# Loads in the order of use, and another share-out of the LayerNorm statistics, at the start of a fused attention and MLP kernel

## Chip, cores, metric

One core of one Trainium2 chip. The metric is device time in microseconds (us). A profiled span is about 1.7 us shorter than the device time of the same execution. All runs named here are single-core runs that were recorded as fast. The experiments ran in three sets of rounds, each set on another chip, always with the kernel before in the same rounds; a comparison across sets is weaker than one within a set.

## The reference, cut to what matters

```python
x  = A_x                                   # 2048 tokens x 1024 channels
xn = layernorm(x)
out = x + attention(xn, wq, wk, wv, wo, beta) + mlp(xn, w1, b1, w2, b2)

def mlp(xn, w1, b1, w2, b2):               # mixes tokens, not channels
    h = layernorm(xn)                      # the second layernorm
    u = gelu(h.T @ w1 + b1)                # 2048 -> 3584
    return (u @ w2 + b2).T
```

Only the start matters here: x is read in 16 chunks of 128 tokens; each chunk needs its mean and variance, a reciprocal square root and a scaling before PE (TensorE) can multiply it by w1. The MLP's contraction runs over tokens, so each chunk of h is one step of a sum that eight PSUM banks hold.

## The kernel before

The first four blocks of 128 hidden units are computed while x is still coming in: for each chunk c, eight matmuls (four w1 blocks, two halves of h) accumulate into the eight banks, 128 "early matmuls" in all. The other 24 blocks follow without a break.

```python
for q in range(4):                                  # loads, all issued by SP
    for c0, n in (((0, 1), (1, 1), (2, 2)) if q == 0 else ((4 * q, 4),)):
        self.load_x(c0, n)                          # 2 KB rows
        if c0 != 2:
            self.load_w1_rows(c0 if q == 0 else 0, q)   # 4 chunks, 256 columns: 512-byte rows
    if q:
        self.load_w1_rows(1, q)
# [...] beta, b1 and b2 are loaded by ACT's queue before that; beta is 64 bytes, sent to all 128 partitions

NORM_ORDER = ("D0 A1 S0 h0 A1' D2 S1 B1 g1 S2 h2 D3 A4 A4' S3 h3 D5 S4,5 D6 B4,5 g4 g5 A7 A7' D8 S6,7 B6,7 g6 g7 "
              "D9 A10 A10' S8,9 D11 B8,9 g8 g9 S10,11 D12 B10,11 g10 g11 A13 A13' D14 S12,13 D15 B12,13 g12 g13 "
              "S14,15 B14,15 g14 g15")
# Dc   statistics of chunk c on DVE: bn_stats, bn_stats, bn_aggr
# Ac   sum on ACT and two small scalings;  Ac'  sum of squares on ACT
# Sc   two small DVE steps, then the square root on ACT
# hc   h of chunk c on DVE;  Bc gc  a bias on DVE, then h on POOL
# [...] the bias columns b1c, b2c are transposed by PE and copied by ACT after S0

for c in range(N_TCH - 2):
    self.early_hidden(c, c + 1, range(8))           # eight matmuls on chunk c
for b in range(8):
    self.early_hidden(N_TCH - 2, N_TCH, (b,))       # chunks 14 and 15, bank by bank
```

Every engine works through its own instructions in this order. A word that stands early in the string can therefore hold up everything behind it on its engine.

The softmax here doesn't subtract the row's maximum and nothing guards it: scores larger than these inputs give would overflow.

## Time and profile before

| | before |
|---|---|
| device time, median | 721.3 us, 3 runs, before the prediction; 721.57 us (720.23 to 722.08, 4 runs: the same three and one more) in the comparison |
| profiled span | 720.2 us |
| first early matmul starts | 10.79 us |
| early matmuls end | 45.48 us |
| x of chunk 1 / of chunks 2 and 3 has landed | 8.22 / 11.16 us |

128 matmuls of 0.216 us are 27.6 us of work, so about 18 of the first 45.5 us are start-up, waiting and slow clock.

The page's head, kernel before: span, then busy time of each engine with its share and its number of instructions. PE is the engine that is always busy.

```profile
span 720.2 us, 11218 instructions
PE 701.0 (97%) x4818; PEld 324.6 (45%) x4818; DVE 263.1 (37%) x577; ACT 276.7 (38%) x314; POOL 111.1 (15%) x151
```

The timeline of PE, kernel before: start, length, engine, line, operation, output<-input, count; in brackets the idle time before and what ended it.

```profile
10.79 1.86 PE L192 MATMUL ps_all<-h,w1s_78 128*128 128x512 bf16 x4 [3.53 <-DVE h L647]
...
23.08 1.02 PE L192 MATMUL ps_all<-h,w1s_78 128*128 128x512 bf16 x4 [2.74 <-POOL h L651]
23.94 1.75 PE L192 MATMUL ps_all<-h,w1s_79 128*128 128x512 bf16 x4
25.48 1.91 PE L192 MATMUL ps_all<-h,w1s_78 128*128 128x512 bf16 x4
...
45.48 13.98 PE L192 MATMUL ps_all<-h,w1s_80 128*128 128x512 bf16 x64
```

Four matmuls take 1.02 us at full clock (the line at 23.08) and 1.7 to 1.9 us at the slow clock that follows the two long waits; it can set in a little later, as here at 23.94. The line at 45.48 is the first of the steady stage (the third w1 tile), so its start is the end of the early matmuls.

The timeline of ACT and DVE, kernel before, three lines:

```profile
8.24 1.06 ACT L615 ACTIVATE junk<-xin 128x1024 bf16<-128x1024 bf16 x1 [5.94 <-DMA xin<-in_A_x_dram]
...
9.98 0.55 DVE L647 TENSOR_SCALAR h<-xin,ln_mv,ln_rs 128x1024 bf16<-128x1024 bf16 x1 [4.25 <-ACT ln_rs L635]
...
32.38 1.01 DVE L633 TENSOR_SCALAR ln_rs<-ln_mv 128x2 f32<-128x2 f32 x1
```

ACT waits for x of chunk 1 until 8.24. The square root of chunk 0 stands behind that in ACT's order, so h of chunk 0 starts at 9.98. The last line is a step on two numbers per partition that takes 0.17 us elsewhere; here it takes 1.01, until the POOL h that was running ends.

The stretches view, kernel before: the stretch and its length, busy time of PE, PEld, DVE, ACT and POOL, granted PE clock, DMA share, GB/s.

```profile
5.00:10.00 5.00, 1.87 (x6) 0.49 (x4) 0.65 (x5) 1.70 (x8) 0.00 (x0) 1.00 0.88 266
...
25.00:30.00 5.00, 5.00 (x19) 2.04 (x18) 4.75 (x12) 2.76 (x7) 3.09 (x4) 0.75 0.21 53
```

From 5 to 10 us every compute engine idles most of the time. From 25 to 30 us PE is always busy, at 0.75 of its clock on average, and DVE is nearly as busy (4.75 of 5 us).

The chain of waits, kernel before (start, length, what):

```profile
2.74 8.42 DMA xin<-in_A_x_dram
...
21.73 1.21 POOL h L651
22.94 0.14 issue
23.08 24.94 PE ps_all L192 x107
```

It goes from the landing of x of chunks 2 and 3 over DVE and ACT to POOL's h of chunk 4, and from 23.08 us on over PE alone.

### The profile page before, as it was taken

Reading aid. Unit: us, or ns where it says so; the run is one execution under the profiler, and the core shown is the slowest. Engines: PE = TensorE matmul, PEld = TensorE weight load, DVE = VectorE, ACT = ScalarE, POOL = GpSimd, SP = SyncE. Lnnn points to the kernel's source line nnn. Section 1 sums busy time; section 2 is a strip of 40 time slices with the busy share of each in tenths; the row PEclk is TensorE's granted clock in tenths of the full one; section 3 lists DMA queues with packets and bytes.
Section 4 is the critical chain, followed back from the end, with each engine's and each line's share of the span. In section 5 each row is a group of like instructions: output and inputs, shape, how many; then the busy total and the mean of one; then the engine's idle time right before and its main releaser. Section 6 shows DMA issues by size and latency. Waiting matters only on the chain.

```text
span 720.2 us, 11218 instructions
## 1 busy us (share of the span) xinstructions
PE 701.0 (97%) x4818; PEld 324.6 (45%) x4818; DVE 263.1 (37%) x577; ACT 276.7 (38%) x314; POOL 111.1 (15%) x151
## 2 busy tenths in 40 slices
PE   6899999999999999999999999999999999999996
PEld 2344444444444444444444444444444444444442
DVE  4970000000002343344444545544555544344452
ACT  4551122111225445445444444443444444434420
POOL 1540000000001112211221111222111122111220
PEclk9999999999999999999999999999999999999999
DMA  9549677246016373872654625355352635527103
GB/s 269 142 115 177 144 190 192 64 112 124 12 60 163 66 125 87 127 118 63 123 117 87 126 44 126 75 109 120 79 125 45 126 86 97 111 53 117 30 27 114
DMA packets 211515, 77.17 MB, mean 107 GB/s; under 512 B 172554, under 2 KB 203274, under 8 KB 211466
## 3 DMA queue, kind: packets, MB, share of 16 engines
q1 hardware_dynamic: 211248, 76.43, 48.9%
q8 instruction: 38, 0.62, 0.4%
q14 instruction: 11, 0.09, 0.0%
q10 hardware_dynamic: 218, 0.02, 0.0%
HBM read 59.79 MB, written 5.24 MB: 90 GB/s over the span
## 4 chain that ended last, share of the span: by engine, by line
PE 93%; DVE 3%; ACT 2%; DMA 1%; issue 1%; SPq 0%; POOL 0%; DVEq 0%; ACTq 0%
PE ps_all L192 93%; DMA xin<-in_A_x_dram 1%; ACT etmp_1584 L749 1%; DVE kT_1570 L746 0%; DVE ln_st L606 0%; DVE kT_1572 L746 0%; DVE kT_1571 L746 0%; DVE ln_st L605 0%; ACT pT L786 0%; SPq L214 0%; DVE h L647 0%; ACT L749 0%; POOL h L651 0%; DVE fin_7771 L1016 0%; DVE fin_7770 L1016 0%
## 5 line engine op out<-in xcount | busy, mean ns | idle before, releaser
L786 ACT ACTIVATE pT<-ps_all 128x1536 bf16<-128x1536 f32 (+1 forms) x96 | 153.0, 1593 | 96.8 <-PE ps_all L192 96.8
L792 POOL TENSOR_SCALAR_AFFINE_SELECT pT<-pT 128x512 bf16<-128x512 bf16 x128 | 90.9, 723 | 561.5 <-ACT pT L786 561.5
L708 ACT ACTIVATE gT<-ps_all,b1c 128x512 bf16<-128x512 f32 x56 | 37.7, 689 | 134.5 <-PE ps_all L192 134.5
L192 PE MATMUL ps_all<-h,w1s_78 128*128 128x512 bf16 x320 | 73.9, 385 | 7.1 <-POOL h L651 3.5
L192 PE MATMUL ps_all<-h,w1s_79 128*128 128x512 bf16 x320 | 73.8, 385 | 0.0
L746 DVE CAST kT_1570<-ps_all 128x512 bf16<-128x512 f32 x11 | 7.6, 690 | 178.9 <-PE ps_all L192 178.9
L192 PE MATMUL ps_all<-gT,w2h_912 128*128 128x512 bf16 x224 | 56.3, 380 | 0.0
L192 PE MATMUL ps_all<-gT,w2h_914 128*128 128x512 bf16 x224 | 56.3, 380 | 0.0
L192 PE MATMUL ps_all<-h,w1s_80 128*128 128x512 bf16 x256 | 55.9, 379 | 0.0
L192 PE MATMUL ps_all<-gT,w2h_913 128*128 128x512 bf16 x224 | 53.9, 381 | 0.0
L192 PE MATMUL ps_all<-gT,w2h_911 128*128 128x512 bf16 x224 | 53.9, 381 | 0.0
L192 PEld LDWEIGHTS ps_all<-h,w1s_78 128*128 128x128 bf16 x320 | 31.4, 99 | 46.3 <-issue 8.5
L192 PEld LDWEIGHTS ps_all<-h,w1s_79 128*128 128x128 bf16 x320 | 31.7, 99 | 39.0 <-issue 2.3
L826 DVE CAST ost_1579<-ps_all 128x264 bf16<-128x264 f32 (+1 forms) x64 | 23.8, 394 | 69.2 <-PE ps_all L192 69.0
L826 DVE CAST ost_1580<-ps_all 128x264 bf16<-128x264 f32 (+1 forms) x64 | 23.8, 394 | 69.0 <-PE ps_all L192 68.9
L192 PEld LDWEIGHTS ps_all<-h,w1s_80 128*128 128x128 bf16 x256 | 25.0, 98 | 30.2
L749 ACT ACTIVATE etmp_1584<-ps_all 128x512 bf16<-128x512 f32 x24 | 14.3, 597 | 58.1 <-DVE kT_1572 L746 20.7
L192 PEld LDWEIGHTS ps_all<-gT,w2h_912 128*128 128x128 bf16 x224 | 20.6, 98 | 25.2 <-issue 2.5
L192 PEld LDWEIGHTS ps_all<-gT,w2h_914 128*128 128x128 bf16 x224 | 20.5, 98 | 24.7 <-issue 2.5
L192 PEld LDWEIGHTS ps_all<-gT,w2h_911 128*128 128x128 bf16 x224 | 19.3, 98 | 25.3 <-issue 6.4
L192 PEld LDWEIGHTS ps_all<-gT,w2h_913 128*128 128x128 bf16 x224 | 19.3, 98 | 25.3 <-issue 6.4
L192 PE MATMUL ps_all<-wo_sb,oT_1587 128*128 128x512 bf16 x128 | 30.2, 379 | 0.0
(154 smaller groups left out, 815.3 us busy)
## 6 DMA issues: line engine op xcount, KB each, us to landing
w1s_80<-in_B_w_dram SPq DMA_DIRECT2D x4, 1024.0 KB, 5.9
w1s_78<-in_B_w_dram SPq DMA_DIRECT2D x4, 1024.0 KB, 5.6
w1s_79<-in_B_w_dram SPq DMA_DIRECT2D x4, 1024.0 KB, 5.7
wq_907<-in_A_wq_dram SPq DMA_DIRECT2D x16, 256.0 KB, 3.5
wq_908<-in_A_wq_dram SPq DMA_DIRECT2D x16, 256.0 KB, 3.6
wk_909<-in_A_wk_dram SPq DMA_DIRECT2D x16, 256.0 KB, 3.8
wk_910<-in_A_wk_dram SPq DMA_DIRECT2D x16, 256.0 KB, 4.0
w2h_911<-in_B_w_dram SPq DMA_DIRECT2D x8, 448.0 KB, 4.8
```

What stands on the lines that cost most here:

```text
L192: ins = self.nc.tensor.matmul(*args, **kwargs)
L708: fw.op("act", lambda e: e.activation(self.gT[:, fc, half * 512:(half + 1) * 512], self.bank(b), ACT.Gelu_apprx_tanh, bias=self.b1c[:, fc: ...
L746: fw.op("dve", lambda e: e.tensor_copy(self.kT[k][:], self.bank(b)), reads=[self.R_bank[b]], writes=[self.R_kT[k]])
L749: fw.op("act", lambda e: e.activation(self.etmp[1][:], self.bank(b), ACT.Exp), reads=[self.R_bank[b]], writes=[self.R_etmp[1]])
L786: fw.op("act", lambda e: e.activation(self.pT[:, :, off:off + total], self.ps[:, 0:4, 0:total], ACT.Exp, scale=SCALE), reads=self.R_bank[0:4],
L792: fw.op("pool", lambda e: e.affine_select(d, d, pattern=[[0, 4], [1, P]], compare_op=ALU.is_ge, fill=0.0, base=0, channel_multiplier=-1), ...
L826: fw.op("dve", lambda e: e.tensor_copy(dst, self.ps[:, b, 0:n * VW]), reads=[self.R_bank[b]], writes=[self.R_ost[o][qb]])
```

## The change

The intent: PE should get its first h earlier, the w1 columns should come with longer rows and in the order in which they are used, and no engine should hold up the chain. Chunks 1, 3, 5, 8, 11 and 14 get their statistics from ACT (before: 1, 4, 7, 10, 13). The first five h and the last one are DVE's, ten h are POOL's (before: 13), and the bias copies move to DVE.

```diff
+        self.w1early = nc.alloc_sbuf_tensor_at("w1early", [P, N_TCH, 512], BF16, offset=w1_at)
@@ loads
-        for q in range(4):
-            for c0, n in (((0, 1), (1, 1), (2, 2)) if q == 0 else ((4 * q, 4),)):
-                self.load_x(c0, n)
-                ...
+        for kind, c0, n in (("x", 0, 1), ("x", 1, 1), ("w", 0, 2), ("x", 2, 2), ("w", 2, 2), ("x", 4, 2), ("x", 6, 2),
+                            ("w", 4, 4), ("x", 8, 4), ("w", 8, 4), ("x", 12, 4), ("w", 12, 4)):
+            if kind == "x":
                 self.load_x(c0, n)
+            else:
+                self.fw.dma(self.w1early[:, c0:c0 + n, :], self.B_w1[c0 * P:(c0 + n) * P, 0:512]...)
@@ bias columns
-            fw.op("act", lambda e: e.activation(col[:], self.bank_bf(b)[:, 0:n], ACT.Copy),
+            fw.op("dve", lambda e: e.tensor_copy(col[:], self.bank_bf(b)[:, 0:n]),
@@ order of work (C: the bias columns)
-    NORM_ORDER = ("D0 A1 S0 h0 A1' D2 S1 B1 g1 S2 h2 D3 A4 A4' S3 h3 D5 S4,5 D6 B4,5 g4 g5 ... g14 g15")
+    NORM_ORDER = ("D0 A1 S0 h0 C A1' S1 h1 A3 D2 S2 h2 A3' D4 S3 h3 A5 S4 h4 A5' D6 S5 B5 g5 S6 D7 B6 g6 A8 A8' S7 D9 "
+                  "B7 g7 S8,9 D10 B8,9 g8 g9 A11 A11' D12 S10,11 D13 B10,11 g10 g11 S12,13 A14 A14' D15 B12,13 g12 g13 "
+                  "S14,15 B14,15 g14 h15")
@@ early matmuls: wait for the w1 rows of the chunk alone, read w1early
```

More of the change, by code (lines that the diff above doesn't have):

```diff
@@ L421, in alloc @@
         self.h = e.take("h", [P, N_TCH, D_MODEL], BF16)
+        w1_at = (e.at + 31) // 32 * 32
         self.w1ring = [e.take(f"w1s{i}", [P, N_TCH, 256], BF16) for i in range(3)]
+        self.w1early = nc.alloc_sbuf_tensor_at("w1early", [P, N_TCH, 512], BF16, offset=w1_at)
         self.late_end = e.at
@@ L516, in consts @@
             self.w1_ring.srcs.append(self.B_w1[:, fp * 256:(fp + 1) * 256].rearrange("(c p) f -> p c f", p=P))
-        self.R_w1q = [[Res(f"w1q{i}_{q}") for q in range(4)] for i in range(2)]
-        for q in range(4):
-            for c0, n in (((0, 1), (1, 1), (2, 2)) if q == 0 else ((4 * q, 4),)):
+        self.R_w1e = [Res(f"w1e{c}") for c in range(N_TCH)]
+        for kind, c0, n in (("x", 0, 1), ("x", 1, 1), ("w", 0, 2), ("x", 2, 2), ("w", 2, 2), ("x", 4, 2), ("x", 6, 2),
+                            ("w", 4, 4), ("x", 8, 4), ("w", 8, 4), ("x", 12, 4), ("w", 12, 4)):
+            if kind == "x":
                 self.load_x(c0, n)
-                if c0 != 2:
-                    i = c0 if q == 0 else 0
-                    self.load_w1_rows(i, q)
-            if q:
-                self.load_w1_rows(1, q)
+            else:
+                self.fw.dma(self.w1early[:, c0:c0 + n, :],
+                            self.B_w1[c0 * P:(c0 + n) * P, 0:512].rearrange("(c p) f -> p c f", p=P),
+                            writes=self.R_w1e[c0:c0 + n])
         self.w1_ring.issued = 2
@@ L548, in load_x @@
                     writes=[self.R_xin[c] for c in range(c0, c0 + n)])
-    def load_w1_rows(self, i, q):
-        rows = self.B_w1[4 * q * P:4 * (q + 1) * P, i * 256:(i + 1) * 256]
-        self.fw.dma(self.w1ring[i][:, 4 * q:4 * q + 4, :], rows.rearrange("(c p) f -> p c f", p=P),
-                    writes=[self.R_w1q[i][q]])
     def late_consts(self):
@@ L571, in late_consts @@
               reads=[self.R_gcol, self.R_gate], writes=[self.R_gate])
-    NORM_ORDER = ("D0 A1 S0 h0 A1' D2 S1 B1 g1 S2 h2 D3 A4 A4' S3 h3 D5 S4,5 D6 B4,5 g4 g5 A7 A7' D8 S6,7 B6,7 g6 g7 "
-                  "D9 A10 A10' S8,9 D11 B8,9 g8 g9 S10,11 D12 B10,11 g10 g11 A13 A13' D14 S12,13 D15 B12,13 g12 g13 "
-                  "S14,15 B14,15 g14 g15")
+    NORM_ORDER = ("D0 A1 S0 h0 C A1' S1 h1 A3 D2 S2 h2 A3' D4 S3 h3 A5 S4 h4 A5' D6 S5 B5 g5 S6 D7 B6 g6 A8 A8' S7 D9 "
+                  "B7 g7 S8,9 D10 B8,9 g8 g9 A11 A11' D12 S10,11 D13 B10,11 g10 g11 S12,13 A14 A14' D15 B12,13 g12 g13 "
+                  "S14,15 B14,15 g14 h15")
     def norm_and_first_hidden(self):
         for word in self.NORM_ORDER.split():
+            if word == "C":
+                self.bias_columns()
+                continue
             kind, cs = word[0], [int(v) for v in word[1:].rstrip("'").split(",")]
@@ L592, in norm_and_first_hidden @@
                 self.scale_h(c, kind == "h")
-            if word == "S0":
-                self.bias_columns()
         self.rstd(0, N_TCH, 0)
@@ L656, in early_hidden @@
         fw = self.fw
-        q = c0 // 4
-        reads = [self.R_w1q[i][q] for i in range(2)] + self.R_w1s[0:2] + self.R_h[c0:c1]
+        reads = self.R_w1e[c0:c1] + self.R_w1s[0:2] + self.R_h[c0:c1]
         with fw.group(reads=reads, writes=[self.R_bank[b] for b in banks]):
@@ L661, in early_hidden @@
                 fc, half = b // 2, b % 2
-                w = self.w1ring[fc // 2]
                 for c in range(c0, c1):
-                    fw.mm(self.bank(b), w[:, c, (fc % 2) * P:(fc % 2 + 1) * P],
+                    fw.mm(self.bank(b), self.w1early[:, c, fc * P:(fc + 1) * P],
                           self.h[:, c, half * 512:(half + 1) * 512], start=(c == 0), stop=(c == N_TCH - 1))
```

## The prediction

> **What bounds the kernel now.** The page gives PE 97% busy of a 720.2 us span, and the chain that ended last is 93% PE. The change touches only the first 45 us; what this stage wins or loses should be shifted into the end time one for one. The timeline of PE: the first matmul on h starts at 10.79 us, chunk 1 follows at 14.98, chunks 2 and 3 end at 20.3, then PE waits 2.74 us for h of chunk 4 (released by POOL) and runs from 23.08 us until the 128 early matmuls end at 45.48. 128 matmuls at 0.216 us are 27.6 us; the other 18 us are start-up, idle or slow clock, the most there is to win.
>
> **Where these go.**
> 1. x of chunk 1 lands at 8.2 us (ACT starts on it at 8.24), amid 512-byte w1 rows; from 4 to 7 us the DMA moves 130 to 145 GB/s, later 310 to 400. ACT is in order, so chunk 0's square root waits behind chunk 1's sums, and h0 starts at 9.98 though its statistics were done at 5.4.
> 2. Later DVE bounds: 4.5 to 4.8 us busy of each 5 between 15 and 35 us. A chunk's statistics cost DVE 1.66 us, a rstd step 0.4, h 0.55; on ACT statistics cost 2.9; POOL's h costs 1.20.
> 3. Small DVE steps (rstd, bias) wait until a running POOL h ends: 0.46, 0.89, 0.62, 1.01 us instead of 0.11 to 0.17. The Trainium skill, page "SBUF — State Buffer" (SBUF: two separate sides), calls the ports that DVE and GpSimd share an exclusive lock for the whole instruction; the trace agrees.
> 4. After idles of 3.5 and 2.7 us matmuls took 0.43 us for about 3.3 us: 1.7 us lost after 23 us. The skill's page "TensorE: Matmul & The Clock Gate" (Part 1) re-throttles after an idle window of about 3.4 us; here 2.74 sufficed.
>
> **What the change does.** x0 and x1 go first, then w1 in 1 KB rows in order of use. A 512-byte packet takes 27 ns, a 2 KB one 84; I estimate 45 for 1 KB, so the early 6 MB get only about 1 us shorter; order matters more. I expect x1 by 5 us, h0 by 7, the first early matmul at 7 to 8.5, chunk 2 at 12 to 13.5. Statistics on ACT rise from 5 to 6 chunks (1.7 us off DVE); five h go to DVE early in place of three (1.1 us on), plus the last one beside POOL's h14, saving about 1 us at the end; POOL's fall from 13 to 10. The bias copies leave ACT.
>
> Placing these durations in the new order by hand, I get h14/h15 at about 35.5 to 37.5 us (before 40.0) and the early matmuls ending at 41 to 43 us instead of 45.48, with short PE gaps (0.4 to 1.9 us), so probably no slow clock. The gain is 2.5 to 5 us, all of it on the critical path.
>
> **Predicted time:** 717.4 us, range 714.0 to 720.2. Chances: faster by over 2% 0.01, within 2% 0.98, slower 0.01.
>
> **Right if:** matmuls on the third w1 tile start near 42 us; the first early matmul before 9; PE's gaps shrink; after that only a shift.
>
> **Wrong if:** x1 or the first w1 rows still land at 8 us or later (h0 stays near 10.5, gain near zero); the one-chunk steps for chunks 5 to 7 make DVE and POOL alternate; many short gaps keep the clock low; or DMA and clock go free and the gain reaches 7 us.

## The result, and the profile after

The changed kernel takes 717.69 us in the median (717.58 to 717.85, 4 runs), against 721.57 us for the kernel before. The ratio is 0.9949, 95% interval 0.9932 to 0.9967. A ratio is the mean time of one kernel's fast runs over that of the other's in the same rounds, so it is not quite the ratio of the medians. The profiled span fell from 720.2 to 716.0 us.

The page's head, changed kernel:

```profile
span 716.0 us, 11137 instructions
PE 693.5 (97%) x4728; PEld 323.9 (45%) x4818; DVE 259.8 (36%) x583; ACT 279.3 (39%) x320; POOL 107.8 (15%) x148
```

Some matmul records are missing in this trace (4728 of 4818), so PE's busy sum is not compared; starts and ends are.

The timeline of PE, changed kernel:

```profile
6.95 3.61 PE L192 MATMUL ps_all<-h,w1early 128*128 128x512 bf16 x16 [0.48 <-DVE b2c L545]
13.15 6.83 PE L192 MATMUL ps_all<-h,w1early 128*128 128x512 bf16 x23 [2.59 <-DVE h L646]
20.92 5.58 PE L192 MATMUL ps_all<-h,w1early 128*128 128x512 bf16 x24 [0.94 <-POOL h L650]
26.65 3.61 PE L192 MATMUL ps_all<-h,w1early 128*128 128x512 bf16 x16 [0.15 <-POOL h L650]
30.85 10.53 PE L192 MATMUL ps_all<-h,w1early 128*128 128x512 bf16 x47 [0.58 <-POOL h L650]
41.22 13.98 PE L192 MATMUL ps_all<-h,w1s_80 128*128 128x512 bf16 x62
```

The early matmuls start at 6.95 instead of 10.79 and end at 41.22 instead of 45.48. That is 4.26 us, and the spans differ by 4.2: what this stage won was handed on whole. Both figures are of one pair of executions; the timed runs of the comparison give 3.7 us (from the ratio). A wait of 2.59 us and a slow clock are still there (the line at 13.15: 24 matmuls, of which 23 have records, take 6.8 us instead of 5.2).

The timeline of ACT and DVE, changed kernel (its line numbers are one lower than before in this part):

```profile
4.33 1.06 ACT L614 ACTIVATE junk<-xin 128x1024 bf16<-128x1024 bf16 x1 [2.03 <-DMA xin<-in_A_x_dram]
...
6.08 0.55 DVE L646 TENSOR_SCALAR h<-xin,ln_mv,ln_rs 128x1024 bf16<-128x1024 bf16 x1 [0.38 <-ACT ln_rs L634]
...
26.70 1.00 DVE L632 TENSOR_SCALAR ln_rs<-ln_mv 128x2 f32<-128x2 f32 x1
```

The stretches view, changed kernel:

```profile
5.00:10.00 5.00, 4.52 (x21) 1.84 (x20) 2.18 (x10) 2.36 (x8) 0.00 (x0) 1.00 0.80 264
```

Between 5 and 10 us the DMA still moves 264 GB/s, as before (266); from 10 to 15 us it moves 380.

The chain of waits, changed kernel:

```profile
2.19 7.93 DMA xin<-in_A_x_dram
...
29.26 0.21 DVE ln_mv L606
29.47 0.04 DVE ln_nb L638
29.50 0.09 issue
29.59 1.21 POOL h L650
30.80 0.05 issue
30.85 1.25 PE ps_all L192 x5
```

This is the finding of the comparison. Before, PE bounded the stage from 23.08 us on. After, the chain stays on DVE (with short visits to ACT) until 29.5 us, and PE bounds only the last 10 us. The chain still begins with x of chunks 2 and 3, which lands at 10.12 us: 7.93 us after its issue, though x0 and x1, with half the bytes each, took 2.8 and 3.1.

The trace of single DMA packets (one record for each piece of a row that is moved) says where that time is. Ten 2 KB packets that start between 4.2 and 4.7 us, when x0 and x1 are in and x of chunks 2 and 3 is on its way, take 1.8 to 2.6 us each; a usual one takes 0.084. The same holds before: in the first 8 us, 20 packets longer than 0.7 us, 24.4 us in sum over 16 DMA engines, and 14 with 25.8 us after. The ACT queue's load of beta, 128 packets of 64 bytes, runs in the same stretch: its packets start between 5.0 and 9.3 us, and the ten long ones end between 6.1 and 7.3. The long ones thus begin up to 0.8 us before beta's first packet; they only end while beta's packets run.

### The profile page after: what moved, and what is told of

The parts are those of the page before. It is cut to its first block, busy times and chain, and to the rows that moved or that the text cites. A ratio compares the mean times of both kernels' runs of the same rounds, so it can differ in the third digit from the quotient of the medians.

```text
span 716.0 us, 11137 instructions
## 1 busy us (share of the span) xinstructions
PE 693.5 (97%) x4728; PEld 323.9 (45%) x4818; DVE 259.8 (36%) x583; ACT 279.3 (39%) x320; POOL 107.8 (15%) x148
## 4 chain that ended last, share of the span: by engine, by line
PE 91%; DVE 4%; ACT 2%; issue 1%; DMA 1%; SPq 0%; POOL 0%; DVEq 0%; ACTq 0%
PE ps_all L192 91%; DMA xin<-in_A_x_dram 1%; ACT etmp_1595 L746 1%; DVE ln_st L605 1%; DVE ln_st L604 1%; DVE kT_1581 L743 0%; DVE kT_1583 L743 0%; DVE kT_1582 L743 0%; ACT pT L783 0%; DVE ln_mv L606 0%; DVE ln_rs L632 0%; ACT L746 0%; SPq L214 0%; POOL h L650 0%; DVE fin_7782 L1013 0%
## 5 line engine op out<-in xcount | busy, mean ns | idle before, releaser
L192 PE MATMUL ps_all<-gT,w2h_925 128*128 128x512 bf16 x211 | 55.0, 380 | 1.0 <-issue 0.5
L192 PE MATMUL ps_all<-h,w1s_80 128*128 128x512 bf16 x251 | 55.6, 379 | 0.3
L192 PE MATMUL ps_all<-h,w1s_79 128*128 128x512 bf16 x251 | 55.6, 379 | 0.3
L192 PE MATMUL ps_all<-h,w1s_78 128*128 128x512 bf16 x250 | 55.6, 379 | 0.3
L192 PE MATMUL ps_all<-gT,w2h_923 128*128 128x512 bf16 x211 | 54.4, 379 | 1.4 <-issue 1.1
L192 PE MATMUL ps_all<-gT,w2h_924 128*128 128x512 bf16 x220 | 53.7, 381 | 0.2
L192 PE MATMUL ps_all<-gT,w2h_922 128*128 128x512 bf16 x221 | 53.6, 380 | 0.3 <-issue 0.2
L192 PEld LDWEIGHTS ps_all<-h,w1s_80 128*128 128x128 bf16 x256 | 25.0, 98 | 30.2
L192 PEld LDWEIGHTS ps_all<-h,w1s_78 128*128 128x128 bf16 x256 | 25.0, 98 | 30.2
L192 PEld LDWEIGHTS ps_all<-h,w1s_79 128*128 128x128 bf16 x256 | 25.0, 98 | 30.2
L192 PE MATMUL ps_all<-h,w1early 128*128 128x512 bf16 x126 | 30.0, 393 | 4.9 <-DVE h L646 2.6
```

The costliest lines, as they stand in the source:

```text
L192: ins = self.nc.tensor.matmul(*args, **kwargs)
```

## The experiments

My theory A: the gain has two parts, earlier landing and a better order of work; after the change DVE is the bound until 31 us, so the clock and the row length are off the critical path. Its rivals are named in each text. Later theory F was added: beta's tiny packets hold up the large ones. Twelve kernels ran. The diffs below are shortened. Where a time in us follows from a ratio, it is (1 - ratio) times the mean of the kernel before in the same rounds.

### Loads alone

The changed kernel with the old order of work:

```diff
-    NORM_ORDER = (new)      bias copies on DVE at C
+    NORM_ORDER = (old)      bias copies on ACT after S0
```

> Only the loads are new; the order of statistics and h is the old one, bias copies on ACT. Theory A (two parts that add up: the earlier landing of x starts the DVE chain about 1 us earlier, the new order of work gives the rest): x1 lands by 4.5 us, first early matmul near 7 to 8 us, chunk 2 and 3 of x near 10.1 us, h of chunk 4 about 1 us earlier than before's 22.9, early matmuls end at 44 to 44.8 us, span about 719.3. Rival B (the loads are the whole gain): end of the early matmuls near 41.2 us, span 716.

Measured: 719.68 us median (718.87 to 721.84), ratio 0.9994 (0.9976 to 1.0013), so 0.4 us. In the profile x1 lands at 4.16 and the first early matmul starts at 8.18, but then PE waits. The timeline of PE, loads alone:

```profile
8.18 1.90 PE L192 MATMUL ps_all<-h,w1early 128*128 128x512 bf16 x8 [1.03 <-DMA w1early<-in_B_w_dram]
14.35 7.87 PE L192 MATMUL ps_all<-h,w1early 128*128 128x512 bf16 x24 [4.27 <-POOL h L650]
```

In the old order the small steps of chunk 1 (S1) stand behind D2 on DVE, so h of chunk 1 waits for x of chunk 2, though x1 was there six us before. This profiled span was 717.9, lower than expected, but other runs of this kernel had spans up to 720.1. The timed gain is under 1 us, as theory A had it. Rival B, that the loads are the whole gain, is out.

### Order of work alone

The kernel before with the new string and the bias copies on DVE; loads as before.

```diff
-    NORM_ORDER = (old)      bias copies on ACT after S0
+    NORM_ORDER = (new)      bias copies on DVE at C
```

> Only the order of statistics and h is new, with the bias copies on DVE; the loads are the old ones. Theory A: h0 stays near 10 us, x2,3 land at 11.2, so the same DVE chain as after the change runs about 1.1 us later: early matmuls end at 42 to 43 us, span about 717.2. Rival B (loads are the whole gain): end near 45.5, span 720.

Measured: 719.22 us median (718.67 to 721.04), ratio 0.9984 (0.9969 to 0.9999), so 1.2 us; profiled span 717.9. x1 lands at 8.01, the first early matmul starts at 10.65. Theory A is right in kind and too high in size: I had expected about 3 us. Which part of the new order counts was not separated, but for the last h (below). Loads and order together look worth more than their sum (0.4 + 1.2): in the same rounds the changed kernel with the filler of the next experiment, which is as fast as the changed kernel, gained 2.8. This surplus of 1.2 us is not shown by the times, since each of the three figures is uncertain by 1.0 to 1.3 us. The trace of the loads alone gives the reason to expect it: the new order can use an early x1, the old one can't.

### Zeros in PE's wait, after the change

```diff
+        k = {2: 11}.get(c0, 0)                      # ahead of chunk 2
+        with fw.group(reads=[self.R_warm], writes=[self.R_bank[0]]):
+            for _ in range(k):                      # adds zero to bank 0
+                fw.mm(self.bank(0), self.warm[:, 0:P], self.warm[:], start=(c0 == 0), stop=(c0 == 0))
```

> The changed kernel with 11 matmuls on zeros put into PE's 2.6 us wait for chunk 2, so that the clock stays fast. Theory A (after the change the chain in this stage runs over DVE until 30.8 us and the slow clock at 13 to 17 us is off it): slow matmuls vanish, the early matmuls still end within 0.3 us of 41.2, span 716 +- 0.4. Rival C (slow clock is still paid): span falls by 1.5 to 1.9 us.

Measured: 717.65 us median (716.92 to 719.04), ratio 0.9961; the median is that of the changed kernel. No slow matmul is left after the first 6 us. The profiled span is 715.2, 0.8 below the changed kernel's and so 0.4 outside what I had allowed: x of chunks 2 and 3 landed at 9.31 in this execution instead of 10.12, and the chain moved by as much. The slow clock after the change costs nothing; rival C is out.

### Zeros in PE's waits, before the change

The same in the kernel before:

```diff
+        k = {0: 15, 1: 10, 4: 11}.get(c0, 0)        # ahead of chunks 0, 1 and 4
```

> The kernel before with matmuls on zeros put into PE's waits for chunks 0, 1 and 4 (15, 10, 11), so that the clock stays fast. Theory A (PE is the bound from 23.08 us on, and the slow clock after the wait is paid): early matmuls end 1.4 to 1.8 us earlier, near 43.9, span about 718.6. Rival D (DVE bounds before as well, down to the last h at 40.0): gain under 0.5 us.

Measured: 720.68 us median (719.63 to 721.25), ratio 0.9999 (0.9985 to 1.0012): no gain. The profiled span was 717.9, which alone would have looked like a success. The timeline of PE of this kernel:

```profile
19.52 2.54 PE L192 MATMUL ps_all<-warm 128*128 128x512 bf16 x11
22.42 25.84 PE L192 MATMUL ps_all<-h,w1s 128*128 128x512 bf16 x116 [0.37 <-POOL h L651]
```

The slow matmuls are gone, and chunk 4 came 0.66 us earlier because x of chunks 2 and 3 had landed 0.64 us earlier in this execution. Six timed runs do not bear out the expected 1.4 to 1.8 us, although the slow clock was gone in all of them: their mean granted clock is 0.997 to 0.998, that of the kernel before in the same rounds 0.990 to 0.995. The number is the one that rival D had forecast, but its reason is not seen: in the profiled execution PE runs without a wait from 22.42 us on. So my reading that the slow clock costs the kernel before 1.7 us holds for the one profiled execution at most. What it costs in a typical run, and how far the filler itself delays PE when h comes early, stays open.

### 512-byte rows in the new order

```diff
-                self.fw.dma(self.w1early[:, c0:c0 + n, :], self.B_w1[rows, 0:512]...)
+                for i in range(2):
+                    self.fw.dma(self.w1half[i][:, c0:c0 + n, :], self.B_w1[rows, i * 256:(i + 1) * 256]...)
```

> The changed kernel with its new order of loads, but each w1 load split into two of 512-byte rows. Theory A (order counts, row length does not, since from 10 us on DVE bounds and not the DMA): span within 0.5 us of the changed kernel's 716.0. Rival E (1 KB rows count): x of the later chunks lands 1 us or more later and the span is 1 us or more longer.

Measured: 716.99 us median (716.59 to 718.21), ratio 0.9948: no slower than the changed kernel. The profiled span of 715.2 is 0.3 below the band, with x of chunks 2 and 3 at 9.40. The 1 KB rows contribute nothing to the gain that these runs can show; what the new loads give comes from their order.

### The last h back on POOL

```diff
-                  "S14,15 B14,15 g14 h15")
+                  "S14,15 B14,15 g14 g15")
```

> The changed kernel with only the last h back on POOL. The prediction had counted about 1 us for it. Theory A (by then PE is behind: the last h on DVE is ready at 35.0 us, POOL's h14 at 36.1, PE wants both near 37.8): span within 0.3 us of the changed kernel. Rival: 0.5 to 1 us longer.

Measured: 717.89 us median (717.48 to 718.54), ratio 0.9959; profiled span 716.2. The same as the changed kernel within the scatter. The 1 us that I had counted for this piece is not there.

This run shows something about the clock as well. The timeline of PE, last h on POOL:

```profile
13.35 1.89 PE L192 MATMUL ps_all<-h,w1early 128*128 128x512 bf16 x8 [2.86 <-DVE h L646]
```

After 2.86 us of idling the clock is full (8 matmuls in 1.89 us). In the changed kernel 2.59 us sufficed to slow it. The clock records of the 14 kept traces say what differs. In each of them the clock changes only on a grid of 3.41 us. On this grid, PE was busy for 5 to 38% of each of the 11 windows at full clock that were followed by half clock, and for 44% or more of every window that was not (2,886 windows at full clock, busy by the matmul records). The 2.59 us fall mostly into one window, which was 35% busy; the 2.86 us are split over two, 66 and 50% busy.

### Beta late

```diff
-        fw.dma(self.beta_sb[:], self.A_beta.partition_broadcast(P), writes=[self.R_beta], issuer="act")
@@ after the last of the early loads, on SP
+        fw.dma(self.beta_sb[:], self.A_beta.partition_broadcast(P), writes=[self.R_beta])
```

> The changed kernel with the load of beta (128 packets of 64 bytes) issued after all big early loads. In the changed kernel x2,3 lands at 10.1 us, though 11 packets of it that start at 4.2 to 4.7 us take about 2 us each. Theory F (beta's tiny packets hold up the 16 engines): those long packets vanish, x2,3 lands at 7.5 to 8.5 us, the DVE chain starts about 2 us earlier, the span falls by 1.5 to 2.5 us. Rival G (the stall is not caused by the tiny packets): x2,3 still near 10 us, span unchanged within 0.4.

Measured: 715.85 us median, five runs from 715.74 to 715.89, ratio 0.9929 (0.9912 to 0.9946). x of chunks 2 and 3 lands at 7.32 us (expected: 7.5 to 8.5). Two packets longer than 0.7 us are left in the first 8 us, 1.8 us in sum instead of 25.8. The stretches view, beta late:

```profile
5.00:10.00 5.00, 4.56 (x20) 1.77 (x19) 3.79 (x13) 3.81 (x12) 0.00 (x0) 1.00 1.01 364
```

364 GB/s instead of 264. The span falls by 1.8 us, and the five runs lie within 0.15 us. (My text speaks of 11 long packets of x; the trace has ten.) Rival G is out: moving beta's load takes most of the stall away. The other traces agree: with the new loads x of chunks 2 and 3 lands at 9.31 to 10.53 us in the five kernels with beta early, and at 7.32 to 8.85 in the five with beta late. Theory F is shown in so far as beta's load is the cause. That the small size of its packets does it is not shown: the edit moved the load in time and to SP's queue at once, and the load also reads the same 64 bytes 128 times.

### No small load at all

Beta late, b1 and b2 not loaded and their columns set to zero (relative error 0.021). Its output is wrong, which doesn't matter for the time.

```diff
-        brow1, brow2 loads, transposes and copies
+        fw.op("pool", lambda e: e.memset(self.b1c[:], 0.0), writes=[self.R_b1c])
+        fw.op("pool", lambda e: e.memset(self.b2c[:], 0.0), writes=[self.R_b2c])
```

> Wrong on purpose in two tiny biases: the changed kernel without the two bias loads (b1 and b2 columns set to zero) and with beta late, so no small load shares the first 20 us. Theory F (all small loads together cause the stall): x2,3 lands at 7.5 to 8.5 us and the span falls by 1.5 to 2.5 us. Rival G: x2,3 still near 10 us, span within 0.4 of 716.0.

Measured: 716.06 us median (715.79 to 717.0), ratio 0.9935; x of chunks 2 and 3 at 8.85, outside the expected 7.5 to 8.5, and the profiled span of 714.7 is 0.2 above the expected band. Taking away the bias loads gives nothing on top of beta's move. Seven packets of 0.8 to 1.5 us remain, so some of the early stalls have another cause, which is not known.

### The kernel before, with beta late

```diff
-        (ACT's queue, first)  beta load
+        (SP, after the last of the early loads)  beta load
```

> The kernel before with nothing but the load of beta moved behind the big early loads. Theory F (beta's tiny packets cause the 2 us packets, which also hold up x of chunk 1 in the kernel before, and their varying length makes its runs scatter over 4 us): x1 lands by 6 us instead of 8.2, x2,3 near 8.5 instead of 11.2, span near 717.5 and its runs scatter by under 1.5 us. Rival G (before's x1 is held up by the 512-byte w1 rows ahead of it, as the prediction had it): x1 still at 8 us, span near 719 to 720 and scattered as before.

Measured: 717.92 us median, five runs from 717.71 to 718.07, ratio 0.9956 (0.9943 to 0.9969). One line moved in the kernel before is worth 3.2 us, not distinguishable from the 3.7 of the whole change under study (the intervals of the ratios overlap), and its five runs scatter over 0.4 us instead of 3.4 in the same rounds. Beta cannot be the only source of scatter: two other kernels with beta late scatter over 1.2 and 1.9 us. The profiled span of 716.3 is 1.2 below the expected one. The timeline of ACT, kernel before with beta late:

```profile
6.79 1.06 ACT L615 ACTIVATE junk<-xin 128x1024 bf16<-128x1024 bf16 x1 [4.49 <-DMA xin<-in_A_x_dram]
```

x1 lands at 6.77 (expected: by 6) and x of chunks 2 and 3 at 8.92 instead of 11.16. The changed kernel has x1 at 4.31, so of the 3.9 us by which x1 comes earlier in the change, 1.45 (8.22 to 6.77) are beta's in this execution, and 2.46 are left for the place in the order.

### Loads alone, beta late

```diff
-    NORM_ORDER = (new)      beta first, on ACT's queue
+    NORM_ORDER = (old)      beta after the early loads, on SP; bias copies on ACT
```

> The new loads with the old order of statistics and h, and beta late: the fourth corner to set beside the kernel before with beta late and the changed kernel with beta late (span 714.2). Theory A (the new order of work is worth about as much as before, 2 us or more, once loads land early): span 716 to 717. Rival H (early landing is all, the order of work does nothing then): span 714.2 +- 0.4.

Measured: 717.44 us median (716.79 to 718.64), ratio 0.995; profiled span 715.8. This fills the table (medians, us):

| | beta early | beta late |
|---|---|---|
| kernel before | 720.51 to 720.94 in these rounds | 717.92 |
| new loads, old order of work | 719.68 | 717.44 |
| new order of work, old loads | 719.22 | not run |
| the change | 717.69 | 715.85 |

With beta late the new order of work is worth 1.6 us on top of the new loads; the new loads alone give 0.5, which is within the scatter of these runs. (The entries of the table are from different rounds.) Rival H is out; theory A's "2 us or more" was a little high. In the profiled execution of this kernel the chain is on PE from 12.25 us on, after a wait of 3.25 us that two windows of half clock (6.8 us) follow. So part of what the new order saves here may be that slow clock; this was not tested.

### Two tries at a better order

The changed kernel with beta late and other strings. In the first DVE makes ten h and POOL six, in the second, other than my expectation says, eleven and five; in both ACT makes seven statistics.

> A try at a better kernel: new loads, beta late, and another order of work (statistics of chunks 1, 3, 5, 9, 10, 14, 15 on ACT; 10 h on DVE, 6 on POOL; small steps of DVE placed so that a POOL h is not running). From the durations of the traces I place the end of the early matmuls 2 to 3 us before the 39.4 of the changed kernel with beta late: span 711.2 to 712.5. If DVE's total or the lock between DVE and POOL bounds instead: 714 or more.

```diff
+    NORM_ORDER = ("D0 A1 S0 h0 C A1' A3 S1 A3' D2 S2 A5 h1 D4 h2 S3 A5' S4 B3 D7 B4 g3 g4 S5 D6 A9 h5 S7 S6 h6 B7 A9' "
+                  "D8 A10 g7 S8 D11 h8 A10' S9 S11 B9 S10 A15 D13 S13 h10 g9 A14 h13 B11 g11 D12 A14' S12 A15' h12 "
+                  "S15 S14 B14 g14 h15")
```

Measured: 713.67 us median (713.58 to 713.97, 4 runs), ratio 0.9898 (0.9883 to 0.9913), correct: 4.0 us faster than the changed kernel, of which about 1.8 are beta's and 2.2 the new string's, and 7.4 us than the one before. The chain of waits, first better order:

```profile
2.19 5.88 DMA xin<-in_A_x_dram
...
13.48 1.21 POOL h L648
14.69 0.05 issue
14.73 33.41 PE ps_all L192 x154
```

The chain reaches PE at 14.73 us instead of 30.85 and does not leave it again; the early matmuls end at 37.19.

> A second order of the same kind (statistics of chunks 1, 3, 5, 9, 10, 11, 14 on ACT; 10 h on DVE, 6 on POOL): span 711.2 to 712.5; 714 or more if DVE's total or the lock bounds.

```diff
+    NORM_ORDER = ("D0 A1 S0 h0 C A1' A3 S1 A3' D2 S2 h1 D4 h2 A5 S3 B3 g3 D6 A5' S5 S4 A10 B5 h4 S6 D8 h6 A9 D7 A10' "
+                  "S7 g5 S8 h7 A9' B8 g8 D12 A11 S9 S10 A11' h9 B10 S12 S11 g10 h11 D15 A14 h12 D13 S15 S13 B15 g15 "
+                  "h13 A14' S14 h14")
```

Measured: 717.4 us median (716.97 to 717.86), ratio 0.995. The profiled span of 715.2 is 2.7 us above the expected band, and the trace says how most of it came about. The timeline of POOL and DVE, second order:

```profile
32.25 3.65 POOL L561 MEMSET vA<- 128x2112 bf16 x2
32.42 3.75 DVE L644 TENSOR_SCALAR h<-xin,ln_mv,ln_rs 128x1024 bf16<-128x1024 bf16 x1 [0.27 <-ACT ln_rs L632]
```

The last h comes after POOL has begun to clear two tiles for a later stage, and it takes 3.75 us instead of 0.55: it ends 0.27 us after the clearing does. PE waits 1.02 us for it at 36.23, then 0.62 us for ACT, and starts the steady stage only at 40.48. In this run 2.14 us of idling were followed by a slow clock as well. The timeline of PE, second order:

```profile
10.91 3.51 PE L192 MATMUL ps_all<-h,w1early 128*128 128x512 bf16 x8 [2.14 <-DVE h L644]
```

## Why the prediction was right, and where it was not

**The total.** Predicted 717.4 us (714.0 to 720.2); measured 717.69.

**"x1 by 5 us, h0 by 7, the first early matmul at 7 to 8.5, chunk 2 at 12 to 13.5".** Measured 4.31, 6.08, 6.95 and 13.15. Right, the first matmul just before its band.

**"h14/h15 at about 35.5 to 37.5 us and the early matmuls ending at 41 to 43".** h15 ended at 35.0, h14 at 36.1, and the early matmuls at 41.22. Right, though h15 came half a microsecond before its band and the end is at the early edge.

**"All of it on the critical path".** Right: 4.26 us in the stage, 4.2 in the span.

**"Amid 512-byte w1 rows".** Half wrong. The change helped x1 because it moved x1 ahead of everything, but the slow stretch from 4 to 7 us was largely beta's load: with the rows left alone and beta moved, the DMA moved 292 GB/s there instead of 140, and x1 came at 6.77. The prediction saw the low GB/s and named the neighbour in the same queue; it never looked at the other queue. In the changed kernel the same stall fell on x of chunks 2 and 3 (10.12 us). The estimate of 45 ns for a 1 KB packet was right (46 in the trace), and the row length did not matter.

**"The last one beside POOL's h14, saving about 1 us at the end".** Mis-sized: with h15 back on POOL the time is 717.89 us, within the scatter. PE comes to chunks 14 and 15 near 37.8 us, later than either engine delivers them (with h15 on POOL, at 37.2).

**"Short PE gaps (0.4 to 1.9 us), so probably no slow clock".** Wrong: one gap was 2.59 us, and the clock slowed. It cost nothing, because PE then waited for h anyway (the filler changed nothing). And "1.7 us lost after 23 us" in the kernel before was read from one execution; filling the waits gained nothing in six timed runs.

**What the total rested on.** The misses touched pieces that are off the critical path after the change: the clock, the last h, the row length. The chain from x of chunks 2 and 3 over DVE was placed with measured durations, and it is the true bound. What the prediction did not see is that another queue set the landing at which the chain begins, and that, by the point estimates, neither the loads nor the order of work alone gives half of the total (0.4 and 1.2 of 2.8 us in the same rounds). That the total came within 0.3 us is in part luck: the kernel before alone scatters over nearly 4 us, and its median was 721.57 us in the comparison but 720.5 to 720.9 in the later rounds.

## What to carry to other kernels

When a load lands late, look at what all queues are doing at that moment, not only at its own queue: a 64-byte load broadcast to 128 partitions delayed megabytes, and moving it was worth about as much as a careful reordering. Look at loads and the order of work together: an early tile is worth nothing to an engine that meets it late in its own order, as x1 of the loads alone shows. A change of about 0.5% must be timed over several runs: one profile showed 2.3 us of gain for the filler that the timed runs did not have.

## What the Trainium skill lacked or had wrong

- "DMA: Bandwidth & Descriptors" (Queues, rings and completion order) says that each DMA engine takes turns between queues packet by packet (a packet there is a group of descriptors; a packet of the trace is one small record), and (Specifications) that transfers under 512 bytes are done as read-modify-write. Neither foretells the size of what was seen: beta's 64-byte packets take 8 to 11 ns each, yet in the stretch in which they run, 2 KB packets of the other queue take up to 2.6 us instead of 0.084, and moving beta gained 1.8 and 3.2 us in two kernels. The mechanism is not shown here.
- "TensorE: Matmul & The Clock Gate" (Part 1) has the clock slow down after at least one idle window of about 3.4 us. Here idles of 2.14 and 2.59 us were followed by slow matmuls (0.43 us each), while one of 2.86 us was not. The page's free-running window fits that the same gap can go either way; a threshold at 3.4 us of idling does not. What the page lacks is how busy a window must be: here half clock followed windows that were up to 38% busy and none that was 44% busy or more; of the ten windows at half clock, two of 50 and 71% were followed by another, eight of 85% or more by full clock.
- "SBUF — State Buffer" (Who interferes with whom) says that whoever takes the pair of ports shared by DVE and GpSimd holds it for the whole instruction. The runs agree, and nothing is lacking here: 1.00 us for a 0.17 us step beside a POOL h. The page names no memset on the GpSimd side; the runs show that one, which only writes, blocks as well: 3.75 us for a 0.55 us h in the second order, and 1.80 us for a copy in the changed kernel that takes 0.18 in the second order, where no memset runs beside it. A reciprocal inside a POOL h took its usual 0.17 us (at 29.71 us in the changed kernel).
